# A fused block-sparse attention and token/channel mixer on one core: gates from fp16 parts, and the second channel product by one level of Strassen's method

## The chip, the cores and the metric

One core of a Trainium2 chip runs the whole program. The metric is the device time of one execution in microseconds (us).

## What is computed

Inputs are q, k and v of shape (4, 8, 768, 64), that is 4 batches and 8 heads, and four weights of the mixer. All are fp32.

1. Attention. Keys lie in 12 blocks of 64. A gate is the product of a query with the mean of a block's keys. Each query keeps its 3 best blocks among those not later than its own, and its own block. Causal softmax attention runs over the kept keys.
2. Mixer, for each batch, on x (768 x 512, the heads side by side): `u = x + (relu(x^T w_tok1) w_tok2)^T` with w_tok1 768 x 256 and w_tok2 256 x 768, then `out = u + relu(u w_ch1) w_ch2` with w_ch1 512 x 1536 and w_ch2 1536 x 512.

```python
k_rep = k.reshape(B, H, n_blocks, block, D).mean(axis=3)
gate_scores = np.einsum('bhsd,bhnd->bhsn', q, k_rep)
...
top_idx = np.argsort(gate_scores, axis=-1)[..., -top_k:]
...
h = np.maximum(xt @ w_tok1, 0.0) @ w_tok2
u = x + h.transpose(0, 2, 1)
h2 = np.maximum(u @ w_ch1, 0.0) @ w_ch2
return (u + h2).astype(np.float32)
```

## The kernel before

Heads are worked in pairs, 16 of them, numbered 0 to 15. Four pairs make a batch. "Gate 5" below means the gate of pair 5.

For one pair the work goes so. Two loads on SP's queue each bring K and Q (`load_qk`), one brings V. TensorE transposes K and Q in fp32 (L359, tiles tkl and tql), and ScalarE (ACT) copies them out of PSUM (`evac_t`, L368). GpSimd (POOL) casts K and Q to fp16 into the augmented operands KA and QA, half the partitions at a time (`cast`, L374), and V (`cast_v`, L280). VectorE (DVE) sums K by blocks (`ksum`, L382) and places the sums (`kcopy`, L390). TensorE makes the gate: five fp32 matmuls, each run as two passes in the trace, of 128 queries against 24 columns, 12 for each head of the pair (`gate`, L400, tile gps). DVE adds a causal bias (`gm`, L408), takes the best eight (L417), and makes a mask (L424, L432), TensorE transposes it (`mask`, L443, tile bps), and DVE puts it beside the queries in QA (`put_mask`, L451), so that the score product carries the mask. For each head follow three score groups (L465), three exponentials on ACT (L478), three multiplications of the diagonal blocks by a triangle on DVE (`diag`, L485, two SBUF tiles in fp16), the product with V (`av`, L496, 21 matmuls of 65 columns, tile aps), a reciprocal (L504) and a normalisation into x16 (L515).

Per batch the mixer runs the token products (L527 and L539, or L558 and L572 for batch 0), `uadd` into u, a transposition of u, the first channel product `ch1` (L608: for each of 12 row chunks 4 matmuls of 512 columns and 4 of 256), relu on ACT (L618) and DVE (L620), the second channel product `ch2` (L629: for each of 6 row blocks 12 matmuls of 512 columns), and `oadd` (L637) with a store of each row block.

The order of the work is not written by hand. Every step is an `Op` with an engine, an assumed length, its dependences and a priority; `plan` places them greedily by their assumed lengths and gives one fixed order, and each engine runs its part of that order first in, first out. PSUM has rings: `big` (2 tiles of two banks, for scores and transposes), `bank` (3) and `av` (1). The mixer of batch 0, and part of batch 1, is laid between the attention of later pairs; batches 1 to 3 mostly follow after the attention. The weights are loaded with a cast on POOL's queue, between its other work (`wq`, `WAIT`): w1 and w2 first, then four pieces each of wc1 and wc2. 120 matmuls on a tile of zeros (L648) keep TensorE at work in the first 17 us of the plan, wherever nothing else is ready; 61 of them are in the program.

`VIA = 16` means that the functions for another way to load K (`load_k8` to `turn_k`) are not used.

Of the kernel before, what the change touches and what calls it, by code (L numbers as in the profile page):

```python
# [9 lines left out]
FP = mybir.dt.float32  # L10
# [18 lines left out]
R = 4  # L29
# [3 lines left out]
VIA = 16  # L33
# [21 lines left out]
class Buf:  # L55


    __slots__ = ("ring", "users", "slot")

    def __init__(self, ring):  # L60
        self.ring, self.users, self.slot = ring, [], None
# [6 lines left out]
def plan(ops, rings, near=60.0):  # L68
# [31 lines left out]
    left = len(ops)  # L100
    while left:
# [7 lines left out]
        for e, cand in ready.items():  # L109
# [7 lines left out]
            for op in cand:  # L117
                t = free[e]
                for d in op.deps:
                    t = max(t, finish(d, e))  # L120
                ok = True
                for buf in op.takes:
                    first = None
                    for s, (_, old) in enumerate(slots[buf.ring]):
                        f = 0.0 if old is None else buf_free(old, e)
                        if f is not None and (first is None or f < first[0]):
                            first = (f, s)
                    if first is None:
                        ok = False
                        break  # L130
                    t = max(t, first[0])
                    buf.slot = first[1]
                if ok:
                    lst.append((t, op))
# [8 lines left out]
        op.start = t  # L143
        for buf in op.takes:
            slots[buf.ring][buf.slot] = (0.0, buf)
# [32 lines left out]
def kernel(  # L178
# [20 lines left out]
    scale = 1.0 / (D ** 0.5)  # L199
    MASKV = -30000.0  # L200
# [9 lines left out]
                 x16=3, h1=2, u=2, uT=2, h2=1, ob=3)  # L210
# [14 lines left out]

    V16 = [sp.tile([128, 2, NJ, 65], F16, tag=f"V{r}", name=f"V{r}") for r in range(R + 1)]
# [3 lines left out]
    K16 = [sp.tile([96, 8, 256], F16, tag=f"K16{y}", name=f"K16{y}") for y in range(2)]  # L230
    ks2 = [sp.tile([128, 2 * NB], FP, tag=f"ks{r}", name=f"ks{r}") for r in range(R)]
    bn16 = [sp.tile([128, NJ, 2, 64], F16, tag=f"bn{r}", name=f"bn{r}") for r in range(R)]
# [3 lines left out]
    wc2_16 = sp.tile([128, NFC, DM], F16, tag="wc2", name="wc2")  # L236
    warm = sp.tile([128, 256], F16, tag="warm", name="warm")
# [46 lines left out]
    def load_k8(i):  # L284
        b, h = pairs[i]

        def f():
            t = sb("kt", [128, 2, 8, D], FP, f"k8_{i}")[0:96]
            T["k8", i] = t
            nc.sync.dma_start(out=t.rearrange("p g t d -> p g (t d)"),  # L290
                              in_=k[b, h:h + 2].rearrange("g (p t) d -> p g (t d)", t=8))
        return f

    def ksum8(i):
        def f():
            t = sp.tile([96, 2, D], FP, tag="kp", bufs=2, name=f"kp_{i}")
            T["kp", i] = t
            nc.vector.tensor_reduce(out=t, in_=T["k8", i].rearrange("p g t d -> p g d t"), axis=AX.X, op=ALU.add)
        return f

    def ksum_pe(i):
        def f():
            p = ps("bank", [128, NB], "kps")
            T["kst", i] = p
            nc.tensor.matmul(out=p, lhsT=T["kp", i].rearrange("p g d -> p (g d)"), rhs=blk, start=True, stop=True)
        return f

    def cast_k8(i):
        def f():
            y = i % 2  # L310
            nc.gpsimd.tensor_copy(out=K16[y].rearrange("p t (g c) -> p g t c", g=4)[:, 0:4:3, :, :], in_=T["k8", i])
        return f

    def store_k(i):
        def f():
            t = dram.tile([S, 256], F16, tag=f"ks{i % 2}", name=f"kscr_{i}")
            T["kscr", i] = t
            nc.sync.dma_start(out=t.rearrange("(p t) c -> p (t c)", t=8), in_=K16[i % 2].rearrange("p t c -> p (t c)"))
        return f

    def turn_k(i):
        return lambda: nc.sync.dma_start_transpose(out=KAX[:, i % R, :, :], in_=T["kscr", i])

    def k16_zero(y):
        return lambda: nc.gpsimd.memset(K16[y].bitcast(FP), 0.0)

    def k16_ind(y):
        def f():
            for c in (64, 128):
                nc.gpsimd.tensor_copy(out=K16[y][:, :, c:c + NB],  # L330
                                      in_=blk.rearrange("p (o n) -> p o n", o=1).broadcast_to([96, 8, NB]))
        return f

# [28 lines left out]
    def evac_t(t32, i):  # L362
        def f():
            name = "qt" if t32 == "ql" else "kt"
            t = sb(name, [128, S if name == "qt" else 1024], FP, f"{name}_{i}")[:, 0:S]
            T[name, i] = t
            p = T["tr", t32, i]
            nc.scalar.copy(out=t, in_=p[:, 0:S])  # L368
        return f

    def cast(dst, name, i, x):
        def f():
            lo = 64 * x
            nc.gpsimd.tensor_copy(out=dst[i % R][x][lo:lo + 64, :], in_=T[name, i][lo:lo + 64, :])  # L374
        return f
# [54 lines left out]
    def bias(i):  # L430
        def f():
            nc.vector.scalar_tensor_tensor(  # L432
                out=bn16[i % R][:, 1:NJ, :, 0:NB],
# [4 lines left out]
    def mask(i):  # L438
        def f():
            p = ps("bank", [128, 128 * GJ], "bps", F16)  # L440
            T["bps", i] = p
            for j in range(GJ):
                nc.tensor.transpose(out=p[:, 128 * j:128 * j + 128],  # L443
                                    in_=bn16[i % R][:, j + 1, :, :].rearrange("p x n -> p (x n)"),
# [157 lines left out]
    def ch1(b, fc, n):  # L602
        def f():
            a, e = CH[n]
            p = ps("bank", [128, e - a], "c1")
# [18 lines left out]
    def ch2(b, j, part, lo, hi):  # L624
# [6 lines left out]
        return f  # L631

# [35 lines left out]
    for i in range(NP):  # L668
# [7 lines left out]

        if i >= VIA:
            kb = Buf("kt")
            ld = op("SP", 500, 0, [], pre - 12, load_k8(i), [kb], size=1400)
            O["ksum", i] = dve(1100, [ld], pre + 1, ksum8(i))  # L680
            nb = Buf("bank")
            O["kpe", i] = pe(115, [O["ksum", i]], pre + 1, ksum_pe(i), [nb])
            O["kcopy", i] = dve(260, [O["kpe", i], O.get(("gate", old))], pre + 1, kcopy(i))
            nb.users.append(O["kcopy", i])
            y = i % 2
            if i < VIA + 2:
                O["kz", y] = op("POOL", 1100, 1150, [], pre - 1, k16_zero(y))
                O["ki", y] = op("POOL", 400, 450, [O["kz", y]], pre - 1, k16_ind(y))
            O["castk", i] = op("POOL", 1150, 1200, [ld, O["ki", y], O.get(("kst", i - 2))], pre + 3, cast_k8(i))
            kb.users += [O["ksum", i], O["castk", i]]  # L690
            O["kst", i] = op("SPO", 600, 0, [O["castk", i], O.get(("cast", "kt", i, 0))], pre + 3.1, store_k(i), size=1600)
            O["kturn", i] = op("SPO", 600, 0, [O["kst", i]] + last_scores(0) + last_scores(1), pre + 3.2, turn_k(i), size=2500)
            O["cast", "kt", i, 0] = O["cast", "kt", i, 1] = O["kturn", i]
        zq = [op("POOL", 880, 930, [], pre - 1, zero_q(i))] if 0 < i < R else []
        for t32, src, off in (("kl", k, 0), ("ql", q, 0.1))[i >= VIA:]:
# [14 lines left out]
            for x in range(2):  # L710
                O["cast", name, i, x] = op("POOL", 770, 825, [O[name, i]] + zq + last_scores(x), pre + 4 + off,
                                           cast(dst, name, i, x))
                tb.users.append(O["cast", name, i, x])
# [207 lines left out]
```

## Time and profile before

| what | value |
|---|---|
| three runs | 272.89, 273.73, 274.72 us; median 273.73 |
| span of the profiled execution, first to last instruction | 270.4 us |
| what the runs show beyond that span | 2.5 to 4.3 us, 3.3 at the median |
| TensorE busy | 262.6 us, 97% |
| VectorE busy | 161.0 us, 60% |
| ScalarE busy | 142.6 us, 53% |
| GpSimd busy | 81.5 us, 30%, nearly all of it before 145 us |
| granted TensorE clock | 1.00 in every slice |

The profiled execution has no time of its own beside its span; the time of a run is set against the span by the third row. An engine's busy time is the union of its instructions' lengths. Instructions overlap a little at their ends, so the length of one is more than the time it adds in a back-to-back stretch. The gates' first matmuls start at 9.6 us (gate 0), 52.65 us (gate 5) and 143.96 us (gate 15); the attention's last product ends near 158 us.

### The profile page before, as it was taken

Reading aid. Unit: us, or ns where it says so; the run is one execution under the profiler, and the core shown is the slowest. Engines: PE = TensorE matmul, PEld = TensorE weight load, DVE = VectorE, ACT = ScalarE, POOL = GpSimd, SP = SyncE. Lnnn points to the kernel's source line nnn. Section 1 sums busy time; section 2 is a strip of 40 time slices with the busy share of each in tenths; the row PEclk is TensorE's granted clock in tenths of the full one; section 3 lists DMA queues with packets and bytes.
Section 4 is the critical chain, followed back from the end, with each engine's and each line's share of the span. In section 5 each row is a group of like instructions: output and inputs, shape, how many; then the busy total and the mean of one; then the engine's idle time right before and its main releaser. Section 6 shows DMA issues by size and latency. Waiting matters only on the chain.

```text
span 270.4 us, 5927 instructions
## 1 busy us (share of the span) xinstructions
PE 262.6 (97%) x2309; PEld 174.5 (65%) x2309; DVE 161.0 (60%) x561; ACT 142.6 (53%) x188; POOL 81.5 (30%) x112
## 2 busy tenths in 40 slices
PE   8899999999999999999999999999999999999994
PEld 5787588877787877776876655544455544465443
DVE  4558968997979777879888533334233252333222
ACT  2367997777888898788487704430024400044100
POOL 8688816763465365336432000000000000000000
PEclk9999999999999999999999999999999999999999
DMA  8999999999999985480741121003920017510032
GB/s 173 205 212 224 189 215 214 197 200 200 213 209 228 212 176 133 103 174 3 158 117 41 39 77 42 0 2 116 260 89 2 0 48 196 153 72 0 2 135 97
DMA packets 94411, 34.67 MB, mean 128 GB/s; under 512 B 85616, under 2 KB 90888, under 8 KB 94384
## 3 DMA queue, kind: packets, MB, share of 16 engines
q1 hardware_dynamic: 90272, 29.89, 50.5%
q0 software_dynamic: 3392, 4.15, 9.1%
q8 instruction: 18, 0.29, 0.5%
q10 hardware_dynamic: 720, 0.25, 0.5%
q14 instruction: 9, 0.07, 0.1%
HBM read 27.21 MB, written 8.65 MB: 133 GB/s over the span
## 4 chain that ended last, share of the span: by engine, by line
PE 87%; DMA 4%; DVE 4%; ACT 3%; issue 1%; SPq 1%; DVEq 0%; ACTq 0%
PE c L629 23%; PE c L608 23%; PE sps L465 12%; PE aps L496 7%; PE gps L400 5%; DMA ql<-in_q_dram 4%; PE tql L359 4%; PE ups L539 3%; PE tkl L359 3%; PE tok L527 3%; ACT e L478 3%; PE bps L443 2%; PE warm L648 1%; PE tok L558 1%; DVE Q L451 1%
## 5 line engine op out<-in xcount | busy, mean ns | idle before, releaser
L478 ACT ACTIVATE e<-sps 128x1024 f16<-128x1024 f32 (+1 forms) x96 | 84.6, 918 | 16.9 <-PE sps L465 12.0
L608 PE MATMUL c<-uT,wc 128*128 128x256 f16 (+1 forms) x384 | 68.1, 326 | 0.2 <-ACT h L618 0.2
L618 ACT ACTIVATE h<-c 128x512 f16<-128x512 f32 x48 | 28.7, 598 | 69.0 <-PE c L608 61.7
L629 PE MATMUL c<-wc,h 128*128 128x512 f16 (+2 forms) x300 | 64.9, 370 | 0.0
L608 PEld LDWEIGHTS <-wc 128*128 128x128 f16 x384 | 37.1, 98 | 24.5 <-issue 0.4
L465 PE MATMUL sps<-Q,KA 128*128 128x512 f16 (+3 forms) x256 | 50.1, 305 | 1.0 <-ACT e L478 0.7
L629 PEld LDWEIGHTS <-h 128*128 128x128 f16 x300 | 28.8, 98 | 31.3 <-issue 0.6
L620 DVE TENSOR_SCALAR h<-c 128x256 f16<-128x256 f32 x48 | 20.2, 420 | 33.8 <-PE c L608 33.8
L637 DVE TENSOR_TENSOR ob<-u,c 128x512 f32<-128x512 f16 (+2 forms) x25 | 16.6, 666 | 38.4 <-PE c L629 38.4
L485 DVE TENSOR_TENSOR e<-e,m 128x256 f16<-128x256 f16 x90 | 31.1, 353 | 12.9 <-ACT e L478 12.2
L374 POOL CAST KA<-kt 64x768 f16<-64x768 f32 x32 | 27.0, 845 | 27.4 <-ACT kt L368 24.2
L465 PEld LDWEIGHTS <-KA 128*128 128x128 f16 x256 | 22.4, 100 | 15.2 <-issue 1.2
L374 POOL CAST Q<-qt 64x768 f16<-64x768 f32 x32 | 26.9, 841 | 10.8 <-ACT qt L368 9.3
L496 PE MATMUL aps<-V,e 128*128 128x65 f16 x672 | 27.0, 193 | 0.1
L496 PEld LDWEIGHTS <-e 128*128 128x128 f16 x672 | 25.6, 98 | 2.2 <-issue 0.4
L400 PEld LDWEIGHTS gps<-ks,qt 128*128 128x128 f32 x160 | 19.2, 192 | 2.4 <-DVE ks L390 1.3
L280 POOL CAST V<-v 128x768 f16<-128x768 f32 x16 | 13.3, 832 | 24.0 <-DMA v<-in_v_dram 19.8
L400 PE MATMUL gps<-ks,qt 128*128 128x24 f32 x160 | 20.0, 267 | 0.3 <-DVE ks L390 0.2
L368 ACT COPY kt<-tkl 128x768 f32<-128x768 f32 x16 | 12.8, 799 | 11.7 <-PE tkl L359 5.9
L515 DVE TENSOR_TENSOR x<-aps,rc 128x384 f16<-128x384 f32 x32 | 17.6, 550 | 0.5
L451 DVE COPY Q<-bps 12x640 f16<-12x640 f16 x32 | 15.5, 484 | 1.9 <-PE bps L443 0.8
L368 ACT COPY qt<-tql 128x768 f32<-128x768 f32 x16 | 12.8, 798 | 6.5 <-PE tql L359 5.7
(55 smaller groups left out, 218.0 us busy)
## 6 DMA issues: line engine op xcount, KB each, us to landing
kl<-in_k_dram SPq DMA_DIRECT2D x32, 192.0 KB, 4.8
ql<-in_q_dram SPq DMA_DIRECT2D x32, 192.0 KB, 4.6
v<-in_v_dram SPq DMA_DIRECT2D x16, 384.0 KB, 5.4
out_dram<-ob SPq DMA_DIRECT2D x23, 256.0 KB, 2.0
wc<-in_moe_w_ch_dram POOLq DMA_DIRECT2D x8, 384.0 KB, 7.4
uscr<-u SPq DMA_DIRECT2D x3, 768.0 KB, 3.7
w<-in_moe_w_tok_dram POOLq DMA_DIRECT2D x2, 384.0 KB, 6.8
out_dram<-ob SPq DMA_DIRECT2D x1, 160.0 KB, 1.8
```

The costliest lines, as they stand in the source:

```text
L359: nc.tensor.transpose(out=p[:, 128 * j:128 * j + 128], in_=t[:, j, :], identity=ident32)
L368: nc.scalar.copy(out=t, in_=p[:, 0:S])
L374: nc.gpsimd.tensor_copy(out=dst[i % R][x][lo:lo + 64, :], in_=T[name, i][lo:lo + 64, :])
L400: nc.tensor.matmul(out=g[:, j, :], lhsT=T["qt", i][:, 128 * j + 128:128 * j + 256], rhs=ks2[i % R], start=True, stop=True)
L465: nc.tensor.matmul(out=p[:, off + a:off + a + n], lhsT=KA[i % R][x][:, 128 * kk:128 * kk + 128], rhs=QA[i % R][x][:, q0 + a:q0 + a + n], s ...
L478: nc.scalar.activation(out=e[:, 0:width], in_=T["sps", i, x, g][:, 0:width], func=AF.Exp, scale=scale)
L485: nc.vector.tensor_tensor(out=d, in0=d, in1=m0, op=ALU.mult)
L496: nc.tensor.matmul(out=p[:, jq, :], lhsT=T["e", i, x, g][:, o:o + 128], rhs=V16[i % (R + 1)][:, x, kk, :], start=(kk == 0), stop=(kk == jq))
L608: nc.tensor.matmul(out=p, lhsT=wc1_16[:, cc, 128 * fc:128 * fc + 128], rhs=T["uT", b][:, cc, a:e], start=(cc == 0), stop=(cc == NCC - 1))
L618: nc.scalar.activation(out=T["h2", b][:, fc, a:e], in_=T["c1", b, fc, n], func=AF.Relu)
L620: nc.vector.tensor_scalar(out=T["h2", b][:, fc, a:e], in0=T["c1", b, fc, n], scalar1=0.0, scalar2=None, op0=ALU.max)
L629: nc.tensor.matmul(out=T["c2", b, j, lo], lhsT=T["h2", b][:, fc, 128 * j:128 * j + 128], rhs=wc2_16[:, fc, lo:hi], start=(fc == 0), stop=( ...
```

## The change

Two things are changed together, and unused code is taken out.

**Gates of pairs 2 to 15.** The evacuation of K and Q now scales by 8 (`UP`). POOL casts a pair's q to fp16 once (`split_q`, tile qh, 128 x 768), takes the rest of queries 128 to 767 in fp16 (`rest_q`, tile qr, 128 x 640, a subtraction of two tiles), and copies qh into the two QA halves, seen as 384 fp32 columns (`place_q`). The block sums are split in the same way on POOL (`split_k`: two copies and two subtractions of 64 x 12), which takes the place of DVE's `kcopy`. The gate is ten fp16 matmuls with 48 columns, qh and qr against both parts of the sums (`gate_parts`), and DVE adds the parts with the bias in two steps (`gm_parts`). The rings bn16 and kp have two buffers, and `bias(i)` waits for `mask(i-2)`.

**Second channel product.** For each of three row blocks j, rows j and j+3 are worked together, and the product is split into 2 x 2 parts, over the inner 12 chunks and the 512 output columns. Seven products of 6 matmuls with 256 columns (`prod`, P1 to P7) take the place of eight. DVE makes four weight sums once (`weight_sum`, 128 x 1536 each), and four half sums for each j (`hsum`, 128 x 768). ACT copies three partial results out of PSUM (`keep`). DVE adds `vsum` and three of the output quarters (`oput`), POOL makes three `vu`, `psum` and the last output quarter (`osum`), all 128 x 256. A row block is stored whole. When no scores are left, channel products may take PSUM tiles of the ring `big` as well. The ring x16 has 2 buffers (3 before) and h1 has 1 (2 before).

The diff, cut to its core:

```diff
-VIA = 16
+SPLIT = 2
+UP = 8.0
...
+                    for ring in [buf.ring] + ([buf.other] if buf.other and not scores_left else []):
...
-                 x16=3, h1=2, u=2, uT=2, h2=1, ob=3)
+                 x16=2, h1=1, u=2, uT=2, h2=1, ob=3, s1=1, s3=1, s4=1, f32=6, qh=2, qr=1)
...
-            nc.scalar.copy(out=t, in_=p[:, 0:S])
+            nc.scalar.mul(out=t, in_=p[:, 0:S], mul=UP)
...
+    def split_q(i):
+            nc.gpsimd.tensor_copy(out=t, in_=T["qt", i])
...
+    def rest_q(i):
+            nc.gpsimd.tensor_tensor(out=t, in0=T["qt", i][:, 128:S], in1=T["qh", i][:, 128:S], op=ALU.subtract)
...
+    def place_q(i, x):
+            nc.gpsimd.tensor_copy(out=QA[i % R][x][lo:lo + 64, :].bitcast(FP), in_=T["qh", i][lo:lo + 64, :].bitcast(FP))
...
+    def split_k(i):
+                nc.gpsimd.tensor_copy(out=t[lo:lo + 64, 1 - x, 0, :], in_=kst[lo:lo + 64, :])
...
+                nc.gpsimd.tensor_tensor(out=t[lo:lo + 64, 1 - x, 1, :], in0=kst[lo:lo + 64, :],
+                                        in1=t[lo:lo + 64, 1 - x, 0, :], op=ALU.subtract)
...
+    def gate_parts(i):
+            for j in range(GJ):
+                for n, t in enumerate((T["qh", i][:, 128 * j + 128:128 * j + 256], T["qr", i][:, 128 * j:128 * j + 128])):
+                    nc.tensor.matmul(out=g[:, j].rearrange("p x c n -> p (x c n)"), lhsT=t,
+                                     rhs=kp[i % 2].rearrange("p x c n -> p (x c n)"), start=(n == 0), stop=(n == 1))
...
+    def gm_parts(i):
+            nc.vector.tensor_tensor(out=cut(t), in0=g[:, :, :, 1, :], in1=cut(gbias), op=ALU.add)
+            nc.vector.tensor_tensor(out=cut(t), in0=g[:, :, :, 0, :], in1=cut(t), op=ALU.add)
...
+    def weight_sum(n):
+            out, a, c = ((t3_16, B22, B12), (B12, B12, B11), (t2_16, B22, B12), (t4_16, B21, t2_16))[n]
+            nc.vector.tensor_tensor(out=out, in0=a, in1=c, op=ALU.subtract)
...
+    def hsum(b, j, n):
+            if n == 1:
+                nc.vector.tensor_tensor(out=T["s", b, j, 1], in0=a21, in1=a22, op=ALU.add)
+            if n == 3:
+                nc.vector.tensor_tensor(out=T["s", b, j, 3], in0=a11, in1=a21, op=ALU.subtract)
+            if n == 2:
+                nc.vector.tensor_tensor(out=a21, in0=T["s", b, j, 1], in1=a11, op=ALU.subtract)
+            if n == 4:
+                nc.vector.tensor_tensor(out=T["s", b, j, 4], in0=a12, in1=a21, op=ALU.subtract)
...
+    def prod(b, j, n, buf):
+            key, x, y, first = {1: ("a", a11, B11, True), 2: ("a", a12, B21, False), 6: ("b", a21, t2_16, True),
+                                7: ("c", T.get(("s", b, j, 3)), t3_16, True), 4: ("c", a22, t4_16, False),
+                                5: ("d", T.get(("s", b, j, 1)), B12, True),
+                                3: ("d", T.get(("s", b, j, 4)), B22, False)}[n]
+            for fc in range(HF):
+                nc.tensor.matmul(out=T["c2" + key, b, j], lhsT=x[:, fc, :], rhs=y[:, fc, :],
...
+    def keep(b, j, key):
+            nc.scalar.copy(out=t, in_=T["c2" + key, b, j])
...
+    def vsum(b, j):
+            nc.vector.tensor_tensor(out=t, in0=T["pa", b, j], in1=T["c2b", b, j], op=ALU.add)
...
+    def vu(b, j, row, col):
+            nc.gpsimd.tensor_tensor(out=t, in0=T["v", b, j], in1=T["u", b][:, j + 3 * row, 256 * col:256 * col + 256], op=ALU.add)
...
+    def oput(b, j, row, col):
+                nc.vector.tensor_tensor(out=o, in0=T["vu", b, j, row, col], in1=T["c2" + "dc"[row], b, j], op=ALU.add)
...
+    def psum(b, j):
+        return lambda: nc.gpsimd.tensor_tensor(out=T["pc", b, j], in0=T["pc", b, j], in1=T["pd", b, j], op=ALU.add)
+    def osum(b, j):
+            nc.gpsimd.tensor_tensor(out=o, in0=T["vu", b, j, 1, 1], in1=T["pc", b, j], op=ALU.add)
...
+                O["qh", i] = op("POOL", 790, 845, [O[name, i]], pre + 2.9, split_q(i), [hb])
+                O["qr", i] = op("POOL", 1450, 1500, [O["qh", i]], pre + 3, rest_q(i), [rb])
...
+                    O["kcopy", i] = op("POOL", 560, 620, [O["ksum", i], O.get(("gate", i - 2))], pre + 1.5, split_k(i))
...
+            O["gate", i] = pe(330, [O["kcopy", i], O["qh", i], O["qr", i]], pre + 2, gate_parts(i), [gb])
```

A part of POOL's order in the built program after the change, around pair 2 (line, operation, tiles, shape):

```
L338 TensorCopy KA<-kt 64x768
L294 TensorCopy V1<-v32 128x12x64
L367 TensorCopy kp0<-kst 64x12 x2
L370 ISA
L370 TensorTensor kp0<-kst,kp0 64x12 x2
L345 TensorCopy qh<-qt 128x768
L338 TensorCopy KA<-kt 64x768
L352 TensorTensor qr<-qt,qh 128x640
L358 TensorCopy Q20<-qh 64x384
L358 TensorCopy Q21<-qh 64x384
```

## The prediction

> **What bounds the kernel now.** I read the page first: busy times, then the chain that ended last.
>
> ```profile
> span 270.4 us, 5927 instructions
> PE 262.6 (97%) x2309; PEld 174.5 (65%) x2309; DVE 161.0 (60%) x561; ACT 142.6 (53%) x188; POOL 81.5 (30%) x112
> PE 87%; DMA 4%; DVE 4%; ACT 3%; issue 1%; SPq 1%; DVEq 0%; ACTq 0%
> ```
>
> TensorE holds 87% of the chain, so PE time taken out comes off the end unless something else steps in. Busy PE is not PE at its peak, so I take paces from the chain in order of time, where merged pieces of back-to-back work stand.
>
> ```profile
> 63.98 0.44 PE c L608 x4
> 72.83 0.67 PE aps L496 x21
> 79.33 1.08 PE gps L400 x10
> 220.04 15.70 PE c L629 x72
> ```
>
> So 108 ns for one pass of a gate (fp32, ten passes a pair), 31.7 ns for an fp16 matmul with 65 columns, 109 ns with 256, and 15.70 us for a batch's 72 products of 512 columns (216 ns each in the merged pieces).
>
> Third, busy time by stretch: from the gate of pair 5 (gate 5) to gate 15, and from there to the end.
>
> ```profile
> 52.65:143.96 91.31, 90.95 (x1014) 68.93 (x1011) 77.42 (x304) 74.53 (x94) 44.31 (x55) 1.00 0.82 160
> 143.96:270.40 126.44, 122.68 (x735) 65.53 (x734) 46.09 (x106) 32.62 (x50) 0.62 (x1) 1.00 0.24 73
> ```
>
> The columns are length, then busy time of PE, PEld, DVE, ACT, POOL, granted clock, DMA share, GB/s. In the attention stretch DVE is busy 77 of 91 us: a second limit close behind PE. In the mixer stretch DVE is a third busy and POOL idle.
>
> **The gates.** Ten passes cost 10 x 0.108 = 1.08 us a pair. Ten fp16 matmuls with 48 columns and a new 128x128 weight each are nearest to the 65-column row, also one weight load per matmul: 0.32 us. Bounds: 31.7 ns, and 98 ns if the weight load (L496 PEld, 98 ns) were not overlapped; I take 31.7, since 21 of them do run in 0.67. Saved 0.76 x 14 pairs = 10.7 us (bound 1.4).
>
> **The products.** 72 x 216 ns = 15.5 us a batch becomes 7 products x 3 row blocks x 6 = 126 matmuls of 256 columns: 126 x 109 ns = 13.7. Saved 1.8 x 4 = 7.2 us. The first channel product already runs 256 columns at this pace with a weight load each. Together **-17.9 us of PE work**.
>
> **DVE.** From the orders I counted the DVE rows between gate 5 and gate 15 and priced them by start-to-start times in back-to-back stretches: diagonal 0.22, Q copy 0.50, block sum 0.86, normalisation 0.47, max 0.08, relu 0.33, small gate steps 0.20, u 0.59. Before: 70.9 us. The change takes out the two kcopy pieces (20 x 0.165 = 3.3) and adds a second gm step (10 x 0.20). Weight sums and half sums are two-operand fp16 work; the diagonal's 256 columns in 0.22 give some 0.55 ns a column, so a half sum of 768 costs 0.47 and a weight sum of 1536 0.87. In this stretch stand 4 weight sums (3.5), 12 half sums (5.6), 8 adds of 256 columns at 0.33 (2.6, against 1.2 of oadds moved out) and smaller shifts: 81.0 us. PE rows there, priced the same way, come to 89.4 before (91.3 measured) and 87.8 after.
>
> DVE also waits for POOL. The diagonal multiply L485 reads two SBUF tiles:
>
> ```profile
> L485 DVE TENSOR_TENSOR e<-e,m x90: 238/284/953, 28.1 to 155.8; 128x256 f16<-128x256 f16 x90
> ```
>
> (count, shortest/median/longest in ns). One of them in the timeline, start and length in us, under two casts on POOL:
>
> ```profile
> 80.29 1.77 POOL L374 CAST Q<-qt 64x768 f16<-64x768 f32 x2
> 80.80 0.52 DVE L485 TENSOR_TENSOR e<-e,m 128x256 f16<-128x256 f16 x1
> ```
>
> Comparing start times, 29 of the 90 start inside a POOL cast and take 502 ns on average; the other 61 take 282. So 0.22 us each, 0.07 over all. POOL's work a pair before is five casts of 0.83 = 4.1 us, half of the 9 us between gates. After: two KA casts and V 2.5, qh 0.83, the two placements of 384 columns 0.41 each (the 64x384 memset row), four 12-column pieces 0.5, and qr, a two-operand op over 640 columns. No POOL row has two operands: at one column per step qr is 0.69 us, at two reads 1.4; I take 1.4. That is 6.1 us of 8.6, with fifteen adds of 256 columns (0.28 to 0.55) for batch 0: 80% busy, 1.6 times the meetings, so 0.125 us for each of 76 two-tile DVE ops. DVE comes to 81.0 + 9.5 = 90.5 us in a stretch where PE needs 87.8. These are 2.7 us; PE's order is fixed and the load uneven, so I take **+4** (0 to 9).
>
> The Trainium skill, "SBUF — State Buffer", section "SBUF: two separate sides", says harsher: one engine holds the shared port pair for its whole instruction, and a DVE op with two SBUF inputs fully blocks. The 502 ns agree in kind. At 80% meetings and half of a 0.85 us op it would be 0.34 us each, DVE 107 us, and the sum 15 us higher.
>
> **A row of unknown price on POOL.** In the built order one ISA row, marked with split_k's line 370, stands ahead of POOL's first two-operand op, for pair 2. Before has none inside the loop. It looks like code that has to be brought in. Its place in the timeline:
>
> ```profile
> 20.54 0.82 POOL L280 CAST V<-v 128x768 f16<-128x768 f32 x1
> 25.02 0.87 PE L359 MATMUL tql<-id,ql 128*128 128x128 f32 x6
> 25.73 0.83 PE L496 MATMUL aps<-V,e 128*128 128x65 f16 x21
> ```
>
> The stretch by engines, and the transfers that POOL issues:
>
> ```profile
> 20.00:30.00 10.00, 9.37 (x113) 7.46 (x112) 8.47 (x41) 7.84 (x10) 8.64 (x12) 1.00 1.13 224
> ...
> w<-in_moe_w_tok_dram POOLq DMA_DIRECT2D x2, 384.0 KB, 6.8
> ```
>
> POOL is free at 21.4. Without the row, four small pieces (0.6), qh 0.83, KA 0.83 and qr 1.4 end at 25.1, just as PE, past the transposes of pair 3's q, comes to gate 2. So all of the row's time is a PE wait: behind gate 2 in PE's queue stand A.V of pair 0 and the scores of pair 1, and ACT and DVE run dry with them. Bounds: ACT's table load, 1.28 us, and two of POOL's transfers from HBM in turn, 14 us; nearest is one such transfer, 6.8 us, with the DMA share at 1.13 there. I take **+7**. The loads of w1 and w2, issued on POOL at 28.3, then come some 10 us later, their users 9: another **+1.5**, since w1 lands with nothing to spare now (0.3 us of wait at L558). The skill's "GPSIMD Engine Reference", section "Instruction dispatch", gives about 6 us for the first call into freshly loaded code; by it the sum is 1 us lower.
>
> **The rest.** The end: the last 192-column add (0.35) and 96 KB store (1.7 to landing) become a 256-column add (0.42) and a 256 KB store (2.0). After the last P6, V (0.5) and five POOL adds of 0.28 to 0.55 end within 3.3 us, while PE still has five products of 0.66: +0.5 (0.4 to 2). ACT gains nine copies a batch (0.39 each, L563's 256 columns) and is busy 82% in the stretch. Scaling in the evacuation, the x16 ring cut to two and bn16 to two: nothing, as their users stand a pair or more ahead; the mixer's half sums: nothing, DVE has 37 us a batch for some 17; were that cover gone, P6 and P3 would wait 0.47 each.
>
> **Sum.** 270.4 - 17.9 + 7 + 1.5 + 4 + 0.5 = 265.5 us of span. The span stands 3.3 us under the median of 273.73 (2.5 to 4.3 over the three runs), so **268.8 us**.
>
> **Rivals.** (1) The ISA row costs next to nothing, as a table load does: 7 less, 261.8. For it: the price is inferred only. Against: it stands there, and early DMA is full. (2) It costs two transfers, 14 us: 275.8. For it: a DMA share over 1 up to 100 us. (3) Slower: the port. Place: DVE's two-tile ops between gates 5 and 15. Price w each: PE waits 81 + 76w - 87.8. From w = 0.21 that is 9 us and the gain is gone: about when every such op meets a POOL op as those 29 do. With qr at 1.4 us, w = 0.25 gives 12.2 instead of 4: 277.0. Against: 61 of 90 meet none now. (4) The gates do not speed up because 48-column matmuls run at weight-load pace: 9.3 lost, 278; the 65-column row speaks against it, and I count it with (3).
>
> **How the numbers follow.** Forecast 0.50 (its own range 264 to 272), (1) 0.20, (2) 0.15, (3) with (4) 0.15. This measurement tells about 1% from no change: 271.0 to 276.5. Faster: 0.42 of the forecast's 0.50 and all of (1), 0.62. Same: 0.08, most of (2) 0.11 and part of (3) 0.04, 0.23. Slower: the rest, 0.15. The range, 260.5 to 276.5, takes in (1) and (2) and leaves the ends of (1) and (3) out.
>
> **What would show it.** In the profile after: the gate's ten passes in 0.3 to 0.4 us; 126 products a batch in 13.7 to 14 us; a hole in POOL and PE of about 7 us near 25; the diagonal (L504 there) at a mean over 353 ns; DVE over 90% between gates 5 and 15 with PE waits on DVE there. No hole makes (1) right; PE waits of over 9 us on DVE make (3) right; gates at 1 us or products over 15 us a batch make the first two steps wrong.

## The result: 3.4% slower, and the profile after

The changed kernel takes **283.0 us** (282.8 to 283.2, four runs) against 273.3 for the kernel before; the ratio is 1.034 [1.031, 1.038] (in brackets the 95% interval). Medians here are over all runs of a kernel, and ratios leave out slow runs, those over 1.5% above the fastest of the same kernel. The prediction, 268.8 us with a range of 260.5 to 276.5, was wrong in sign. What happened is of the kind of rival (3), and larger.

The head of the page after: span, busy times, and the chain of work that ended last.

```profile
span 280.8 us, 6646 instructions
PE 250.9 (89%) x2513; PEld 183.5 (65%) x2513; DVE 212.2 (76%) x620; ACT 154.1 (55%) x224; POOL 167.9 (60%) x255
DVE 38%; PE 35%; POOL 11%; DMA 7%; issue 5%; ACT 3%; SPq 0%; POOLq 0%; DVEq 0%; ACTq 0%
```

PE is busy 11.7 us less and the span is 10.4 us longer. PE's share of the chain fell from 87% to 35%; DVE holds 38%. POOL's busy time doubled.

Busy time by stretch, cut at gates 5 and 15 as in the prediction (length, then PE, PEld, DVE, ACT, POOL, granted clock, DMA share, GB/s):

```profile
0.00:56.79 56.79, 46.53 (x550) 36.78 (x551) 39.98 (x146) 35.39 (x45) 44.22 (x80) 1.00 1.14 207
56.79:164.47 107.68, 94.47 (x1099) 69.38 (x1097) 102.66 (x318) 77.40 (x102) 82.87 (x125) 0.98 0.66 129
164.47:280.80 116.33, 109.91 (x869) 77.32 (x866) 69.52 (x158) 41.35 (x79) 40.80 (x52) 0.99 0.25 78
```

The first stretch lost 4.1 us, the second 16.4 (107.7 for 91.3), the third gained 10.1. In the second DVE is busy for 102.7 of 107.7 us.

Some of DVE's and POOL's groups of instructions (count, busy us, mean ns, idle before them):

```profile
L504 DVE TENSOR_TENSOR e<-e,m 128x256 f16<-128x256 f16 x90 | 44.2, 500 | 3.0 <-ACT e L497 2.7
L443 DVE TENSOR_TENSOR lt<-gm,m 128x120 f32<-128x120 f32 x16 | 7.2, 451 | 0.1
L534 DVE TENSOR_TENSOR x<-aps,rc 128x384 f16<-128x384 f32 x32 | 17.6, 549 | 0.4
L352 POOL TENSOR_TENSOR qr<-qt,qh 128x640 f16<-128x640 f32 x14 | 20.0, 1428 | 0.9
L713 POOL TENSOR_TENSOR vu<-v,u 128x256 f32<-128x256 f32 x36 | 27.8, 799 | 49.4 <-DVE v L706 49.0
```

The diagonal multiply has gone from a mean of 353 ns to 500 and `lt` from 278 to 451; both read two SBUF tiles. The normalisation, which reads one tile from PSUM and one from SBUF, stays where it was (550 and 549). The subtraction `qr` takes 1.43 us, and a 256-column add on POOL 0.80.

One place in the timeline shows it (start, length, in us; the last brackets are idle time before; dots stand for rows left out):

```profile
134.98 1.71 POOL L352 TENSOR_TENSOR qr<-qt,qh 128x640 f16<-128x640 f32 x1
135.36 1.47 DVE L443 TENSOR_TENSOR lt<-gm,m 128x120 f32<-128x120 f32 x1
...
137.36 1.76 POOL L338 CAST KA<-kt 64x768 f16<-64x768 f32 x2
137.48 0.90 DVE L451 SCALAR_TENSOR_TENSOR bn<-lt,own 128x120 f16<-128x120 f32 x1
...
138.43 0.47 PE L462 MATMUL bps<-id,bn 128*128 128x128 f16 x5 [2.90 <-DVE bn L451]
```

`lt` alone takes 0.28 us. Here it starts 0.4 us into `qr` and ends 0.14 us after it; the next small step starts just inside the first of two casts of K and lasts until that cast is done. Behind it PE stands idle for 2.90 us before the mask's transposes, with the scores queued behind them.

### The profile page after: what moved, and what is told of

Same layout as the page of the kernel before. It is cut to its first block, busy times and chain, and to the rows that moved or that the text cites. A ratio compares the mean times of both kernels' runs of the same rounds, so it can differ in the third digit from the quotient of the medians.

```text
span 280.8 us, 6646 instructions
## 1 busy us (share of the span) xinstructions
PE 250.9 (89%) x2513; PEld 183.5 (65%) x2513; DVE 212.2 (76%) x620; ACT 154.1 (55%) x224; POOL 167.9 (60%) x255
## 4 chain that ended last, share of the span: by engine, by line
DVE 38%; PE 35%; POOL 11%; DMA 7%; issue 5%; ACT 3%; SPq 0%; POOLq 0%; DVEq 0%; ACTq 0%
PE c L627 18%; DVE e L504 9%; POOL vu L713 5%; DVE u L566 4%; PE sps L484 4%; DMA ql<-in_q_dram 4%; DMA wc<-in_moe_w_ch_dram 3%; DVE m L436 3%; DVE x L534 3%; PE c L691 2%; DVE kst L401 2%; PE aps L515 2%; PE tok L546 2%; DVE Q L470 2%; ACT e L497 2%
## 5 line engine op out<-in xcount | busy, mean ns | idle before, releaser
L713 POOL TENSOR_TENSOR vu<-v,u 128x256 f32<-128x256 f32 x36 | 27.8, 799 | 49.4 <-DVE v L706 49.0
L504 DVE TENSOR_TENSOR e<-e,m 128x256 f16<-128x256 f16 x90 | 44.2, 500 | 3.0 <-ACT e L497 2.7
L731 POOL TENSOR_TENSOR pc<-pc,pd 128x256 f32<-128x256 f32 x12 | 9.4, 786 | 24.9 <-ACT pd L699 24.9
L691 PEld LDWEIGHTS <-s 128*128 128x128 f16 x216 | 20.8, 98 | 4.0 <-issue 0.5
L332 ACT ACTIVATE kt<-tkl 128x768 f32<-128x768 f32 x16 | 13.0, 811 | 15.4 <-PE tkl L323 7.9
L691 PE MATMUL c<-t,h 128*128 128x256 f16 x144 | 20.2, 279 | 0.7 <-ACT pc L699 0.6
L352 POOL TENSOR_TENSOR qr<-qt,qh 128x640 f16<-128x640 f32 x14 | 20.0, 1428 | 0.9
L691 PE MATMUL c<-wc,h 128*128 128x256 f16 x144 | 19.6, 272 | 0.7 <-ACT pa L699 0.6
L691 PE MATMUL c<-wc,s 128*128 128x256 f16 x144 | 19.6, 272 | 0.0
L358 POOL COPY Q<-qh 64x384 f32<-64x384 f32 x28 | 17.5, 625 | 1.1
```

The lines of the kernel that those rows point to most:

```text
L352: nc.gpsimd.tensor_tensor(out=t, in0=T["qt", i][:, 128:S], in1=T["qh", i][:, 128:S], op=ALU.subtract)
L504: nc.vector.tensor_tensor(out=d, in0=d, in1=m0, op=ALU.mult)
L691: nc.tensor.matmul(out=T["c2" + key, b, j], lhsT=x[:, fc, :], rhs=y[:, fc, :], start=first and fc == 0, stop=fc == HF - 1, skip_group_chec ...
L713: nc.gpsimd.tensor_tensor(out=t, in0=T["v", b, j], in1=T["u", b][:, j + 3 * row, 256 * col:256 * col + 256], op=ALU.add)
```

## The experiments

All ratios are against the kernel before in the same session; a difference of two ratios is turned into us with 273.4. "The diagonal" is the multiply by the causal mask (L504 after, L485 before). A step of DVE that reads two SBUF tiles is called a two-tile step.

Every edit passes through the planner. The traces of e1_gates, e5_short_qr, e9_pieces and e16_short_set have the same order of work on PE, DVE and ACT, and so have the changed kernel and e10_after_short: within each of these two sets only what POOL does in the place of the subtraction differs. The other runs have an order laid anew, and part of their difference can come from that; e11_before_sub, e14_before_pieces and e15_before_set share one such order, which is not that of the kernel before.

**Each part alone.** First cut: the change with the plain second product (e1_gates), and the change with all gates in float32 (e2_strassen: `SPLIT = 16`).

> Only the fp16 gates; the second channel product is that of the kernel before. Theory P (in the attention DVE is the bound: added rows, and waits of its two-tile ops for POOL): the gates add POOL's qr (1.4 us a pair) but almost no DVE rows, so DVE's rows stay near 70 us and its waits grow by some 0.15 us for each of 80 two-tile ops, 82 in all, about what PE then needs (91.3 - 7.6 = 83.7); part of the gates' 10.7 us arrives: 266 to 270 us. Theory Q (nothing is wrong in the attention; POOL's 256-column adds hold up the product phases): the whole 10.7 arrives, 262 to 263. Theory G (the gate waits for qh and qr on POOL, whose order is too long): slower than before, 276 or more, with PE waits at L386.

> Only Strassen's products; all gates are those of the kernel before. Theory P: batch 0's weight sums, half sums and adds (11 us of DVE rows) bring DVE near PE's 89 us in the attention but POOL has less to do than in the changed kernel, so the diagonal stays under 420 ns: the attention loses 2 to 5 us, the products gain 7.2 at most, less what POOL's adds take: 271 to 276. Theory Q: the loss of 9.7 us and the gates' lost 10.7 are here: 290 or more. Theory G: 266 to 268, all of the loss being with the gates.

Gates alone: 277.0 us, 1.013 [1.009, 1.018]. Strassen alone: 274.9 us, 1.006 [1.004, 1.009]. Each part by itself is slower than before. The gates do the larger harm. P expected part of their gain and Q all of it. Only G had the time, 276 or more, but not by its reason: PE waits for the subtraction 1.3 us in all at the gates of e1_gates, and 4.6 us for DVE's `bn` alone. The diagonal's mean is 477 ns with the gates alone and 388 with Strassen alone, DVE's waits for POOL thus coming mainly with the gates. Strassen alone lies where P had it (271 to 276, diagonal under 420 ns).

**The diagonal on PE.** One constant, on both kernels, takes the 90 multiplies off DVE and gives PE twelve more matmuls a pair:

```
-TRI = 1
+TRI = 16
```

> The changed kernel with the diagonal's causal mask added by PE in every pair (12 more matmuls of 128 columns a pair, 15 pairs, 54 ns each: 9.7 us of PE) in place of 90 multiplies on DVE (44 us there). Theory P: DVE falls far below PE, which then sets the attention at 87.8 + 6.5 us between gates 5 and 15; as that stretch takes about 110 us now, the kernel gets faster in spite of the added PE work: 270 to 278 us. Theories Q and G: PE's work comes on top: 290 to 293.

> The same edit on the kernel before, as a control. There PE is the bound, so by theory P the 9.7 us of PE come on top, 281 to 284 us. If the kernel before were already held by DVE in the attention, it would stay at 273 or get faster.

On the kernel before it costs 2.9% (281.2 us, 1.029 [1.025, 1.033]): PE was the bound. On the changed kernel 280.4 us, 1.028 [1.021, 1.035], no slower than without it (1.034 [1.031, 1.038]): the same PE work is paid for by what DVE gains, as P says, but the time lies between P's 270 to 278 and the 290 to 293 of Q and G. POOL's share of the chain is 26% there; something on POOL also counts.

**Which part of the gates.** Four edits: the subtraction over 16 of its 640 columns (on the gates alone and on the whole change); the gate no longer waiting for it; K's copies moved from POOL to ACT. Where the subtraction is short or unread, part of the gate sum is left out, so these runs are tests and not kernels to use.

```
# e5_short_qr, e10_after_short: qr0 is a zeroed tile
+nc.gpsimd.tensor_tensor(out=qr0[:, 0:16], in0=T["qt", i][:, 128:144], in1=T["qh", i][:, 128:144], op=ALU.subtract)
# e6_unread_qr
-O["gate", i] = pe(330, [O["kcopy", i], O["qh", i], O["qr", i]], ...
+O["gate", i] = pe(330, [O["kcopy", i], O["qh", i]], ...
# e7_k_by_act: two copies from PSUM, and the block sum from PSUM
+nc.scalar.mul(out=KA[i % R][x][lo:lo + 64, :], in_=T["tr", "kl", i][lo:lo + 64, 0:S], mul=UP)
```

> The gates alone (as in e1_gates), but the rest of q is formed for 16 of its 640 columns, the others left at zero, so that part of the gate sum is left out; POOL's subtraction falls from 1.41 us to some 0.25. Theory P: 7 of the 90 diagonal multiplies began inside that subtraction and took 831 ns instead of 278, and some small steps too: DVE wins 5 to 8 us of its waits, and the time falls from 277 to 270 to 273 us, with the diagonal's mean at 420 ns or less. If only the path to the gate counts (theory G): the same or faster, but with the diagonal still at 470. If neither counts: 276 to 278.

> The gates alone, POOL's work unchanged, but the gate's second matmul reads the high part a second time, so that no gate waits for the rest of q (its value is left out of the sum). Theory P (POOL's load on the port): nothing changes, 275.5 to 278 us, diagonal near 477 ns. Theory G (the path q, high part, rest, gate is too long): the gate's waits go, and most of the lost 10 us come back: 266 to 270.

> The gates alone, with K's fp16 copies written by ACT straight from PSUM (two copies of 64 partitions a pair in place of one of 128; 0.8 us more of ACT a pair) and the block sum read from PSUM: POOL loses its two KA casts a pair (27 us in all). Theory P: the 13 diagonal multiplies that began in a cast (907 ns) and half a dozen small steps are free: DVE wins 8 to 12 us, 266 to 271 us. The rival is that ACT (72% busy in the attention) or the two large PSUM buffers, which are now held for two copies, take the place: 276 to 282.

> The whole change, with the rest of q formed for 16 of 640 columns only (that part of the gate sum is left out). In e5_short_qr the same edit to the gates alone gave 11 us back, as much as DVE's busy time fell. If the subtraction costs the whole change as much: 270 to 274 us, which leaves DVE's added rows of batch 0 as the rest of the miss (268.8 was predicted). If the added rows of the products alone had filled DVE: 279 or more.

With the short subtraction the gates alone take **265.8 us**, 0.971 [0.966, 0.976]: 4.2 points, 11.6 us, under e1_gates, and three quarters of the gain that was promised for them. The whole change with it takes 270.5 us, 0.987 [0.982, 0.992]: 13 us less than as it stands. So one POOL instruction, fourteen times 1.4 us, decides the sign, in an order of work that is otherwise the same. DVE's diagonal in e1_gates and e5_short_qr (the second trace is of that kernel's longest run, 268.7 us):

```profile
L504 DVE TENSOR_TENSOR e<-e,m 128x256 f16<-128x256 f16 x90 | 42.3, 477 | 6.6 <-ACT e L497 6.6
```
```profile
L504 DVE TENSOR_TENSOR e<-e,m 128x256 f16<-128x256 f16 x90 | 30.8, 349 | 8.9 <-ACT e L497 8.6
```

The gate's own wait for the subtraction is not it: it is 1.3 us in e1_gates. Without that wait (e6_unread_qr) the time is 279.3 us, 1.022 [1.018, 1.026], longer than with it, though in an order laid anew, where PE waits 3.9 us at the gate for `qh`; why it is longer was not followed up. Moving K's copies to ACT (e7_k_by_act) made it 280.4 us, 1.024 [1.019, 1.029], for a reason of its own: ACT's copies and DVE's block sum, now readers of one PSUM buffer, took turns (ACT KA waited 9.6 us for DVE kst and DVE kst 9.2 us for ACT KA), and POOL waited 50.7 us for the block sums. It says nothing on the port.

**How the subtraction harms.** In pieces, then in pieces with the gate freed, then in pieces with the planner told POOL's real prices:

```
# e9_pieces
+for a in range(0, S - 128, 128):
+    nc.gpsimd.tensor_tensor(out=t[:, a:a + 128], in0=T["qt", i][:, a + 128:a + 256], ...
# e13_pieces_plan, also 430 -> 540 and 560 -> 880
-op("POOL", 1450, 1500, [O["qh", i]], pre + 3, rest_q(i), [rb])
+op("POOL", 2200, 2260, [O["qh", i]], pre + 3, rest_q(i), [rb])
```

> The gates alone, with the rest of q formed by five subtractions of 128 columns instead of one of 640; nothing is left out. In e1_gates a diagonal multiply that began inside the long subtraction was let go when it ended, up to 1.98 us later when a cast stood just ahead of it. Theory L (a DVE step with two SBUF tiles waits to the end of the POOL instruction that is running, no longer): pieces of some 0.45 us each bring the mean of those that begin in the subtraction from 831 to under 550 ns, and the time to 268 to 273 us, although POOL works 0.6 to 0.9 us a pair longer. Theory T (what counts is how long POOL is busy in all, since pieces with no wait between them leave DVE no gap): 277 to 281 us, diagonal at 480 ns or more.

> The gates alone, the rest of q in five pieces as in e9_pieces, and the gate's second matmul reading the high part as in e6_unread_qr (the rest's value is left out of the sum). Theory B (the subtraction harms twice, and either harm alone is enough: in one piece it holds DVE's two-tile steps, in five it is 0.8 us longer and PE waits for it at the gate, L382, 4 to 7 us): with both taken away while POOL still does all of its work, 266 to 270 us. Theory S (POOL works in order, and what is queued behind the subtraction, the copies of K and Q, comes late): no change, 275 to 279.

> e9_pieces with the planner told what POOL's steps take: 2200 ns for the rest of q (1450 before), 880 for the four block sum pieces (560), 540 for a placement (430). The planner then puts PE's gate later in the order. Theory B: PE waits less at the gate, and since DVE's waits are already short, 268 to 273 us. Theory S, or if the gate's lateness is only handed on to the mask and the scores behind it: 275 to 279.

Theory L was right on DVE and wrong on the time. A diagonal that begins inside the subtraction lasts 430 ns on average instead of 831, and DVE's busy time falls from 172.5 to 163.6 us; yet the kernel takes 276.9 us, 1.009 [1.005, 1.012], hardly less than in one piece. Five pieces of 441 ns are 2.2 us instead of 1.41, and now PE waits (engine waiting, releaser; total us, times, longest) in e9_pieces:

```profile
PE gps L382 <- POOL qr L353: 4.0, 21, 0.4
```

With the gate freed of that, in another order (e12_pieces_unread: 275.4 us, 1.006 [1.003, 1.009], where S had it), PE waits for the next thing in POOL's queue, the high part `qh` of the following pair:

```profile
PE gps L382 <- POOL qh L345: 4.9, 4, 3.1
```

With true prices in the plan (e13_pieces_plan) 274.3 us, 1.000 [0.996, 1.004]: the plan wins 2.4 us over e9_pieces, and the gates bring nothing. So DVE's waits are not the only way (e9_pieces shows it, with e1_gates' order and less of these waits): POOL works in order, and its lateness is a second one.

**Port against queue.** "Port" stands for the first way, in which a reading POOL instruction and a two-tile step of DVE shut each other out, and "queue" for the second, in which POOL's own work comes late. To tell the two apart POOL was kept busy with memsets, which read nothing. On the kernel before, a subtraction that nobody reads was added for each pair, whole and in pieces, and then memsets in its place; on the gates alone, memsets behind the short subtraction.

```
# e11_before_sub; e14_before_pieces does the same in five pieces
+nc.gpsimd.tensor_tensor(out=qx, in0=T["qt", i][:, 128:S], in1=qx, op=ALU.subtract)
# e15_before_set, behind a copy of 16 columns; e16_short_set, behind the short subtraction
+for n in range(4):
+    nc.gpsimd.memset(qx.bitcast(FP), 0.0)
```

> The kernel before with one subtraction over 640 columns (float32 and fp16 in, fp16 out) added to POOL for each pair from 2 on, right after the evacuation of q; nothing reads it. POOL was busy 44 of 91 us in the attention, so its own queue has room. Theory P: some diagonal multiplies wait behind it, DVE's busy time rises by 8 to 12 us in a stretch where it had about 14 us to spare beside PE, so the time rises by 3 to 8 us: 276 to 281. If an idle engine's work were free: 273 to 274.

> The kernel before with the unread subtraction of e11_before_sub in five pieces of 128 columns: POOL is busier than there (31 us added instead of 20), and again nothing waits for the result. Theory L (DVE is held for the length of the running POOL instruction): DVE's busy time rises by 2 to 5 us instead of 9, and the time is 274 to 277 us, against 281 with one piece. Theory T or S (POOL's time in all counts): 281 or more.

> The kernel before with the same place on POOL filled as in e11_before_sub, but by one copy of 16 columns and four memsets of 128x320 float32 (some 0.35 us each by the 64x384 memset's 0.41), 1.6 us a pair, which read nothing. The few small DVE steps that began inside a POOL memset took 282 to 284 ns, no longer than alone. Theory P (what costs is that DVE's steps with two SBUF tiles and POOL's reading instructions shut each other out): no change, 273 to 276, diagonal near 353 ns. Theory S (POOL's time counts, since its own copies come late): 280 to 283 as in e11_before_sub.

> The gates alone with the rest of q formed for 16 columns only (e5_short_qr; that part of the gate sum is left out) and four such memsets behind it, so that POOL is as long busy as in e1_gates. Theory P: as e5_short_qr, 265 to 269 us. Theory S: as e1_gates, 275 to 279.

The group in e16_short_set, and its diagonal:

```profile
L355 POOL MEMSET qx<- 128x320 f32 x56 | 20.4, 364 | 2.4
L507 DVE TENSOR_TENSOR e<-e,m 128x256 f16<-128x256 f16 x90 | 32.1, 363 | 8.8 <-ACT e L500 8.6
```

A diagonal that begins inside a memset is not held by it: in e15_before_set 18 of them took 288 ns on average, against 286 for those that begin outside POOL's memsets and casts. In e16_short_set 14 of 16 took 284 ns; the other two began 11 and 5 ns before a memset's end, with a copy of q right behind it, and lasted 0.60 us. On the gates e16_short_set takes 270.1 us, 0.986 [0.982, 0.990]. POOL is busier there than in e1_gates (118 us against 115), and it is 7.4 us faster; it is 4.2 us slower than e5_short_qr, where POOL has 18 us less. DVE's busy time goes with the reading instruction alone: 172.5 us in e1_gates, 161.5 in e16_short_set, 161.3 in e5_short_qr. So of the 11.6 us about **two thirds come from instructions that read SBUF and hold DVE's two-tile steps, one third from POOL being late** with its own work (the gate's wait for the subtraction, 1.3 us, falls in the first part). Neither theory alone stands.

On the kernel before, the subtraction and the memsets cost the same: 281.1 us, 1.024 [1.019, 1.029] with the subtraction, 283.9 us, 1.034 [1.025, 1.042] in pieces, 280.6 us, 1.024 [1.019, 1.029] with memsets. There P fell. What the traces show is POOL's queue again, since the mixer's weights are fetched from it. POOL's timeline in the kernel before (three of the transfers it issues):

```profile
28.34 0.86 POOL L660 DMA_DIRECT2D w<-in_moe_w_tok_dram  x1
43.45 1.07 POOL L663 DMA_DIRECT2D wc<-in_moe_w_ch_dram  x2
60.97 1.51 POOL L665 DMA_DIRECT2D wc<-in_moe_w_ch_dram  x2
```

and in e15_before_set:

```profile
30.86 0.86 POOL L668 DMA_DIRECT2D w<-in_moe_w_tok_dram  x1
48.80 1.07 POOL L671 DMA_DIRECT2D wc<-in_moe_w_ch_dram  x2
67.79 1.51 POOL L673 DMA_DIRECT2D wc<-in_moe_w_ch_dram  x2
```

and one of its windows:

```profile
30.00:40.00 10.00, 7.58 (x96) 5.29 (x93) 4.62 (x16) 6.83 (x9) 6.14 (x10) 0.85 1.26 217
```

The transfers leave 2.5 to 6.8 us later, PE waits 2.0 us for `w1`, and the granted clock of that window is 0.85. That wait is 2.0 of the 6.6 us lost, and the clock can account for 1.7 more (3.41 us at half of it, see the last section). The step added on POOL also changes the order of all engines, in the same way in these three runs, and a worse order is a rival that no run here excludes. So the cause of the loss on the kernel before stays open, and how that of e11_before_sub divides was not measured.

**Where Strassen fits, and remedies.** Batch 0's product lies in the attention, where DVE is full; batches 1 to 3 lie behind it. e8_later keeps the plain product for batch 0 and forms the weight sums after it. e17_v_by_act is the gates alone with V's copy moved from POOL to ACT, from SBUF to SBUF. e18_both joins the two.

```
# e8_later: before Strassen's loop over j
+if b == 0:
+    ...
+    for n in range(4):
+        TW.append(dve(880, h2b.users + TW[-1:], 1500.0 + n, weight_sum(n)))
+    continue
# e17_v_by_act
-nc.gpsimd.tensor_copy(out=V16[i % (R + 1)][:, :, :, 0:D], in_=T["v32", i])
+nc.scalar.copy(out=V16[i % (R + 1)][:, :, :, 0:D], in_=T["v32", i])
```

> All gates of the kernel before; Strassen's products for batches 1 to 3 only, batch 0's second channel product as before and the weight sums after it. Theory P (the harm is done to DVE in the attention, where batch 0's work lies): the attention is that of the kernel before, and each of the three later batches gains 1.6 us as their product phases do in the changed kernel (14.2 us of PE for 15.8): 268 to 270 us. Theory Q (POOL's adds of 0.8 us hold up these phases): 273 to 276.

> The gates alone, whole, with V's fp16 copy made by ACT from SBUF (0.8 us a pair more on ACT) instead of by POOL, which loses 16 reading casts of 0.84 us. No PSUM buffer is held for it. Both theories P and S: about 13 of the 16 us that e5_short_qr took off POOL, so 267 to 271 us, if ACT's 72% in the attention leave room. The rival: ACT, whose exponentials feed everything, becomes late: 276 or more.

> Both parts of the change, whole, with two things moved: V's fp16 copy is made by ACT (e17_v_by_act) and Strassen's products are used for batches 1 to 3 only, with the weight sums after batch 0 (e8_later). If the two gains add: 271.3 of e17_v_by_act less the 2.8 of e8_later, 268 to 270 us, 1.3 to 2% under the kernel before. If the one eats the other's room (ACT's nine copies a batch, POOL's adds): 271 to 273.

e8_later: 270.6 us, 0.991 [0.988, 0.994], so batch 0 alone turned Strassen from a gain of 0.9% into a loss of 0.6%. e17_v_by_act: 271.3 us, 0.991 [0.987, 0.994], 6.2 us under e1_gates. Its diagonal's mean falls only from 477 to 456 ns, so shorter waits of DVE explain little of this; how the rest divides between POOL's queue and the new order was not separated. **e18_both: 268.9 us, 0.982 [0.978, 0.985]**, faster than both kernels. The gains add, as expected. Its page and its attention:

```profile
span 267.0 us, 6485 instructions
PE 52%; DVE 24%; POOL 10%; issue 4%; DMA 4%; ACT 4%; SPq 1%; POOLq 0%; DVEq 0%; ACTq 0%
60.00:165.00 105.00, 102.18 (x1136) 69.67 (x1134) 93.49 (x316) 88.00 (x114) 57.94 (x98) 1.00 0.66 137
```

PE is again busy nearly all the time in the attention (102.2 of 105 us), and POOL is busy 55% of it, where the changed kernel has 77% between gates 5 and 15.

## Why the prediction was wrong, point by point

**The gates: right in price, short in effect.** The matmuls start 26 ns apart (seven steps between these two) where 31.7 was taken:

```profile
25.78 0.18 PE L380 MATMUL gps<-kp,qh 128*128 128x48 f16 x1
...
25.96 0.18 PE L380 MATMUL gps<-kp,qr 128*128 128x48 f16 x1
```

With the subtraction out of the way the gates bring 8.0 us (e5_short_qr) of the 10.7 promised. Rival (4) is dead.

**The products: right in price, half in effect.** Six of 256 columns take 0.66 us (the last ones start at 273.96, 274.61 and 275.27), as priced. Three batches bring 2.5 us (e8_later) of 5.4. Part went into the end: behind the last product POOL adds twice more, 0.72 us each, and 4.8 us pass from PE's last matmul to the end of the span against 3.5 before; +0.5 was taken, +1.3 came. POOL's adds, taken at 0.28 to 0.55 us, measure 0.80 on average. ACT's copies were put at nothing, and in e8_later PE waits 1.2 us for them in the products.

**The ISA row: wrong, 8.5 us too much.** Taken at +7 and +1.5 for the weights behind it; it cost nothing that the trace shows, and rival (1) was right on it:

```profile
21.42 0.44 POOL L367 CAST kp<-kst 64x12 f16<-64x12 f32 x2
21.95 0.48 POOL L370 TENSOR_TENSOR kp<-kst,kp 64x12 f16<-64x12 f32 x2
```

The Trainium skill's "GPSIMD Engine Reference", section "Instruction dispatch", gives about 6 us for the first call into freshly loaded code, and this is not seen here either. The row stands in the trace as MODIFY_POOL_CONFIG at 21.8 us, and 0.09 us lie between POOL's row before it and its first two-operand pieces; whether code was loaded no run shows.

**DVE and POOL: the step that failed.** The sum had +4 (0 to 9) for the stretch from gate 5 to gate 15; it got 16.4 us longer. PE's work there was priced at 1.6 us less than before; PE is in fact busy 3.5 us more (94.5 for 91.0) and idle 12.9 us more, and 11.2 us of its idle time are waits for DVE, of which the kernel before has 0.2 us in its stretch (the changed kernel from 56.79 to 164.47 us; total us, times, longest):

```profile
PE bps L462 <- DVE bn L451: 6.6, 6, 2.9
PE aps L515 <- DVE e L504: 1.8, 4, 0.8
PE sps L484 <- DVE Q L470: 1.6, 3, 1.1
PE aps L515 <- DVE x L534: 1.2, 2, 0.7
```

POOL's load was judged well (80% taken, 77% measured), its subtraction too (1.4 us taken, 1.43 measured), and the number of meetings nearly: 46 of 90 diagonals by the factor 1.6, 56 measured (0.07 times 1.6 is 0.11, so the 0.125 of the sum was already a little above its own working). What was off is above all the price of a meeting. It was carried over from the kernel before, 0.22 us, where the POOL instructions met are casts of 0.8 us. Those that begin in a POOL instruction now take 635 ns against 277 outside, 0.36 us each, and those that begin inside the subtraction 1140. Over all diagonals that is 0.22 us where 0.125 was taken. The other two-tile rows follow: `lt` and `bn` 0.17, a half sum 0.55 undisturbed (0.47 taken) and 0.71 on average, the four weight sums 0.94 to 2.35 (0.87 taken). All in all 97 two-tile steps stand in the stretch, where the sum had 76, and against their undisturbed lengths they lose 0.23 us each, 22.2 us together, where the sum had 9.5. Without these waits DVE's 102.7 us are 80.5, close to the 81.0 of the sum: the rows were priced well, and the waits are the term that failed. By its own signs rival (3) had come true (w over 0.21, PE waits on DVE over 9 us); its 277.0 us was still too low, for it took 76 steps and knew DVE's waits only.

The prediction weighed the Trainium skill's "SBUF — State Buffer", section "SBUF: two separate sides", and left it for the milder row. Its estimate by that page's rule, one owner of the shared pair for a whole instruction, was 0.34 us for each two-tile step, DVE at 107 us and the sum 15 us higher, which makes 283.8 us. Measured are 0.23 us and 102.7 us, between the two prices. That 283.8 lies so near 283.0 is partly luck: it still holds 8.5 us for the ISA row, and nothing for POOL's lateness. In kind the traces agree with the rule, and also with what the same section says of its limit, that a DVE operation with two SBUF inputs meets only a GpSimd operation that reads SBUF: the diagonals inside a memset took 288 ns against 286.

**What no step had.** POOL was costed as a burden on DVE and never as a queue that others wait for: the pieces and the memsets show that its time alone costs, 4.2 us in the gates. The prediction did follow POOL's order up to gate 2, and not beyond. And batch 0's half and weight sums went into a stretch that the sum itself had filled to the brim; promised 1.8 us, they cost 4.2 (e2_strassen against e8_later), 6.0 off.

Added up: 2.7 short on the gates, 2.9 on batches 1 to 3, 6.0 on batch 0, 13.0 for the subtraction, less 8.5 + 4 + 0.5 that the sum had laid aside and that are contained in these or did not come, is 11.6 of the 14.2 us missed. The other 2.6 us are there without the subtraction too: e10_after_short gains 3.6 us, where the gates (8.0 gained), batches 1 to 3 (2.5 gained) and batch 0 (4.2 lost) add up to 6.3. Why the parts cost more together was not traced.

## What to carry to other kernels

When work moves to an engine that looks idle, price it twice: by which of the busy engine's instructions it shuts out (here two SBUF operands against a reading POOL instruction, for as long as that instruction lasts), and by who stands behind it in its own queue. Where a second limit lies at 85% of the stretch, an edit that takes work from the first and gives a little to the second is worth what is left between them, and the same edit placed in another stretch can be worth its full price. Let a test of the doubtful instruction decide before the large edit is built: filling POOL with a dummy for one run on the kernel before (e11_before_sub, 2.4% slower) would have given a warning.

## What the runs showed of the hardware that was not expected

- A two-tile DVE step that meets a run of POOL instructions with no gap may not get in between: in e1_gates three diagonals that began in a cast with the subtraction right behind it lasted 1.68, 1.92 and 2.26 us, through both.
- Cutting POOL work up is expensive: 128 columns take 441 ns (e9_pieces) where 640 take 1414 (e1_gates), and 12 columns of 64 partitions still 223 to 251 on average in the changed kernel.
- Some holes in PE's work go with a lower granted clock, which is 1.00 in every window of the kernel before: 0.83 in 30:40 of e9_pieces, 0.85 in the same window of e15_before_set, and in the changed kernel about the 2.90 us wait shown above as follows. In each it is one stretch of 3.41 us at 0.50. It begins as the hole ends in the changed kernel (at 138.75 us, a hole of 2.90 us) and in e15_before_set (at 36.96 us, a hole of 2.01 us), but in e9_pieces (at 34.23 us) only five waits of 0.16 to 0.41 us at the gate lie ahead of it. A hole of 1.86 us at 51.6 us of the changed kernel has no such stretch behind it. That a hole causes it was not tested.

```profile
130.00:140.00 10.00, 6.96 (x78) 5.55 (x77) 9.96 (x27) 5.97 (x9) 9.46 (x15) 0.94 0.82 194
140.00:150.00 10.00, 8.59 (x101) 6.19 (x100) 9.69 (x33) 6.25 (x8) 7.85 (x13) 0.89 0.14 52
```
